# Pooled attention and a maxout network on one Trainium2 core: scores one slot later in three blocks, weight differences by halves, and the last block's lower output stored in two column halves by two queues

## Chip, core and metric

The kernel runs on one core of a Trainium2 chip (trn2). The metric is the device time of one execution in microseconds (us), the median of several runs; lower is better. A profile was taken of one further execution, with the time of every instruction and of every DMA packet.

## What is computed

Attention with keys and values averaged over groups of 8, and then a network whose hidden layer is the maximum of three products:

```python
B, H, S, D = q.shape                                  # 8, 8, 576, 64; pool = 8, Sp = 72
k_p = k.reshape(B, H, Sp, pool, D).mean(axis=3)
v_p = v.reshape(B, H, Sp, pool, D).mean(axis=3)
scores = scale * np.matmul(q, k_p.transpose(0, 1, 3, 2))
attn = softmax(scores)
x = np.matmul(attn, v_p)      # (0, 2, 1, 3), reshaped to 4608 tokens x 512
h = np.maximum(np.maximum(x @ w1, x @ w2), x @ w3)    # w: 512 x 768
out = h @ w_out                                       # 768 x 512
```

## The kernel before

**Work on two levels.** The attention goes by batch: there are 8 batches of 576 tokens. The network goes by blocks of 512 tokens, `n` = 0 to 8. While block `n` goes through the network, the attention of batch `n` + 1 is woven between its matmuls, so TensorE (PE) always has something to do.

**The maximum.** The kernel computes the hidden layer as relu and max of two differences: `w2 - w1` and `w3 - w1` stand in the tiles `mw1` and `mw2` in place of `w2` and `w3`, and the part that is linear in `x` is taken through a third matrix, `wm` = `w1` times `w_out`. The differences are made by `sub_w` (L315 to L320) on VectorE (DVE), in place, one call for 256 columns of both. The hidden layer uses columns `jc` by 128: a call `d1` (columns 256 to 511) serves `jc` = 2 and 3, and `d2` serves `jc` = 4 and 5. `sub_w` takes a start and an end in units of 128 columns; before the loop of block 0 it is already called by halves for the first 256 columns (L483 to L486).

**Slots.** `hidden` (L363) and `project` (L381) are generators, and each `yield` ends a slot. In blocks 2 to 4 a block has 20 slots: slots 0 to 11 are the hidden layer (for each of 6 `jc`, a slot of four 512-column matmuls for `mw1`, evicted by a Relu on ScalarE (ACT), and a slot for `mw2`, evicted by a maximum on DVE, L354), and slots 12 to 19 the projection of four tiles of 128 tokens, in two slots each. The eight slots of block 0 whose `jc` is 0 or 1, and the four whose `jc` is 2, take 256 tokens instead of 512. The PSUM tiles `pw` of the slots rotate through three buffers.

**What is put between slots.** `block` (L498) runs a slot and then the steps that a plan gives for it. `plan` (L532) is the plan of blocks 2 to 4. `k` turns the pooled keys of the next batch (`turn_k`, L194): three transposes on PE into one PSUM tile `pkt`, and four copies into the two zero-padded tiles `kz`, for these batches two by DVE (first tile, `par` = 0) and then two by ACT (second tile, `par` = 1), L198. `s0` to `s7` are the scores of the eight heads (`scores`, L217): for each head one matmul of 320 columns and one of 256, one with each tile of `kz`, and an exponential over 576 columns on ACT (L212). `v0` to `v4` multiply by the values (`values`, L251) and `x` puts the result into `xT` with a DMA transpose. `T` loads transposed queries. In block 0 the plan is written out at L510: it has `d1` after slot 6 and `d2` after slot 10.

**Order.** The order of every engine is the order in which the program issues: the kernel switches the scheduler off with `manual_schedule`. An instruction that has to wait holds back what stands behind it on its engine.

**GpSimd (POOL)** pools the keys and values of the batches 1 to 7 (`fold_v`, and `fold_k` but for batch 1) and issues the loads.

**The end.** The last blocks use a scheme of seven products in place of eight (`seven`, `out_seven`). For the output, `out_seven` (L660) computes a block of 512 tokens as two token halves `j` and two column halves, `lo` and `hi`, in the tile `ob`, and `m` counts the two groups of 128 tokens in each half. The products of the last block (`LAST` = 8) come in the order of L864: 1, 2, 6, 7, 5, 3, 4. The half `j` = 1 (the lower output) is complete in its right columns once products 5 and 7 are added (DVE, `plus`, L725), and in its left columns once product 3 is copied (ACT, L722). `store` (L667) writes a half of one `j` or all its columns, in two DMAs, one for each 64 partitions:

```python
if i in (5, 7, 3) and ended(5, 7, 3):
    store(nc.sync, 1, slice(0, C))
if n == LAST and i in (2, 4) and ended(i):
    store((nc.gpsimd, nc.sync)[i // 4], 0, (lo, hi)[i // 4])
```

After the last product comes what was left of the projection of block 6: one tile of 128 tokens in two column halves (L387), the left one evicted by ACT (L400) and the right one by DVE (L398), each stored by one DMA from SyncE (SP) and one from ACT (L404).

Of the kernel before, what the change touches and what calls it, by code (L numbers as in the profile page):

```python
# [14 lines left out]
def kernel(  # L15
# [11 lines left out]
    nc = tc.nc  # L27
# [3 lines left out]
    B, H, S, D = q.shape  # L31
# [127 lines left out]
    def fold_k(b, e, i0=0, i1=6):  # L159
        if b not in kps:  # L160
            new_kp(b)
        fold(e, kts[b][:, i0:i1], kps[b][:, i0:i1], F16 if e is nc.vector else F32)
# [12 lines left out]
    def turn_q(b, n0, n1, evac, tag):  # L175
        if b not in qTs:
            qTs[b] = sb2.tile([128, 2 * NG, 128], BF16, name="qT", tag="qT")
        pqt = psum([128, n1 - n0, 128], BF16, name="pqt", tag=tag[0],
                       bufs=tag[1])
        qf = qbs[b].rearrange("p hp t d -> p (hp t d)")  # L180
        for n in range(n0, n1):
            nc.tensor.transpose(pqt[:, n - n0, :], qf[:, 128 * n:128 * n + 128],
                                ident)
        evac(out=qTs[b][:, n0:n1, :], in_=pqt)
# [9 lines left out]
    def turn_k(b):  # L194
        pkt = keys(b, ATT if len(pools) < 3 else SC)
        for par, evac in enumerate((nc.vector.tensor_copy, nc.scalar.copy)):
            for odd in range(2):
                (evac if b > 2 else nc.vector.tensor_copy)(  # L198
                    out=kz_all[b % 2][par][64 * par:64 * par + 64, :, 0:Sp].rearrange(
                         "p h (r i t) -> p h r i t", i=3, t=2)[:, :, :, :, odd],  # L200
                     in_=pkt[64 * odd:64 * odd + 64].rearrange("p i (h r) -> p h r i", r=12))
# [12 lines left out]
    def new_et(b):  # L214
        ets[b] = sb2.tile([Sp, H, S], F16, name="et", tag="et")
# [62 lines left out]
    def do(b, steps):  # L278

        for name in steps.split():
            i = int(name[1:] or 0)
            if name[0] in "qQ":
                turn_q(b, *QS[i], nc.vector.tensor_copy if name[0] == "Q"
                       else nc.scalar.copy, TR)
            elif name[0] == "T":
                qTs[b] = sb2.tile([128, 2 * NG, 128], BF16, name="qT", tag="qT")
                nc.sync.dma_start_transpose(
                    out=qTs[b], in_=qbs[b].rearrange("p hp t d -> p (hp t d)"))  # L290
            elif name[0] == "k":
                turn_k(b)
            elif name[0] == "K":
                fold_k(b, nc.vector)
            elif name[0] == "s":
                if i == 0:
                    new_et(b)
                (scores if len(pools) < 3 else scores_flat)(b, i)
            elif name[0] == "d":
                sub_w(i)  # L300
            elif name[0] == "z":
                for par in range(2):
                    nc.vector.memset(kz_all[1][par], 0.0)
            elif name[0] == "w":
                turn_w(i, nc.scalar.copy if i % 2 else nc.vector.tensor_copy)
            elif name[0] == "v":
                xns[b, i] = values(b, CHUNKS[i][0])
            else:
                turn_x(b, *CHUNKS[i], xns[b, i], TR if b == 1 else ATT,
                       nc.vector.tensor_copy if name[0] == "X" else nc.scalar.copy)  # L310
# [4 lines left out]
    def sub_w(i, j0=0, j1=2, wi=(1, 2)):  # L315

        part = slice(256 * i + 128 * j0, 256 * i + 128 * j1)
        for t in [w_sb[w] for w in wi]:
            nc.vector.tensor_tensor(out=t[:, :, part], in0=t[:, :, part],  # L319
                                    in1=w_sb[0][:, :, part], op=ALU.subtract)  # L320
# [211 lines left out]
    def plan(n):  # L532
        b = n + 1
        got = {0: [(b, "k")]}
        got.update({2 + h: [(b, f"s{h}")] for h in range(H)})
        got.update({12 + c: [(b, f"v{c} x{c}")] for c in range(5)})
        got[14 if n == 2 else 13].append((b + 2, "T"))
        return got
# [70 lines left out]
    LAST = TOK // NB - 1  # L609
# [50 lines left out]
    def out_seven(n):  # L660

        o = sb2.tile([128, 2304], F32, name="ob", tag="et")[:, 0:2048].rearrange(
            "p (j m c) -> p j m c", j=2, m=2)
        lo, hi = slice(0, HALF), slice(HALF, C)
        banks, done = {}, set()

        def store(e, j, c):  # L667
            for u in range(2):
                b, g = divmod(2 * (4 * n + 2 * j) + u, NG)
                pair = g + 2 < NG and GS[g + 2] == GS[g] + 4  # L670
                for m in range(0, 2, 1 + pair):
                    b, g = divmod(2 * (4 * n + 2 * j + m) + u, NG)
                    dst = out[S * b:S * b + S, :].rearrange("(r g) c -> r g c", g=NG)
                    e.dma_start(out=dst[:, GS[g]:GS[g] + 4 * pair + 1:4, c],
                                in_=o[64 * u:64 * u + 64, j, m:m + 1 + pair, c])

        def bank(of, m):
            if n < LAST:
                if of not in banks:
                    if of == "A":  # L680
                        banks["A"] = psum([128, 2, 2, HALF], F32, name="oA", tag="val",
                                          bufs=1)[:, 0]
                    else:
                        tag = (PO, SC)[of == "C"]
                        banks[of] = psum([128, 2, HALF], F32, name=f"o{of}", tag=tag[0],
                                         bufs=tag[1])
                return banks[of]
            if (of, m) not in banks:
                tag = {"A": PA, "B": SC, "C": BC if m == 0 else SC}[of]
                banks[of, m] = psum([128, 2, HALF], F32, name=f"o{of}", tag=tag[0],  # L690
                                    bufs=tag[1])[:, 0:1]
            return banks[of, m]

        def product(i, *ms):
            for m in ms:
                matmuls(i, m)
            done.update((i, m) for m in ms)
            evict(i, ms)

        def matmuls(i, m):  # L700
            of = "B" if i == 2 else "C" if i in (4, 7) else "A"
            p = bank(of, m)[:, m if n < LAST else 0]
            za, zb = PRODUCTS[i]
            for r in range(5):
                c = slice(128 * m, 128 * m + 128)
                if isinstance(zb, str):
                    z = int(zb[1]) - 1
                    left = turns(n)[:, z, r, c] if r < 2 else th[n][z][:, r - 2, c]
                else:
                    at = HALF * (zb % 2) + 128 * m  # L710
                    left = (xT[:, 2 * (zb // 2) + r, NB * n + at:NB * n + at + 128] if r < 2
                            else hTs[n][:, JH * (zb // 2) + r - 2, at:at + 128])
                right = out_s(int(za[1]))[:, r] if isinstance(za, str) else out_w(za, r)
                nc.tensor.matmul(  # L714
                    p, left, right, stop=(r == 4), skip_group_check=True,
                    start=(i in FIRST and r == 0 and (m == 0 or n == LAST)))

        def evict(i, ms):
            m, at = ms[0], slice(ms[0], ms[-1] + 1)

            def copy(j, c):
                nc.scalar.copy(out=o[:, j, at, c], in_=bank("A", m))  # L722

            def plus(j, c, of):
                nc.vector.tensor_tensor(out=o[:, j, at, c], in0=o[:, j, at, c],  # L725
                                        in1=bank(of, m), op=ALU.add)

            def ended(*parts):
                return all((z, k) in done for z in parts for k in range(2))

            if i in (1, 5, 6, 3):
                copy(int(i in (5, 3)), lo if i in (1, 3) else hi)
            elif i == 2:
                plus(0, lo, "B")
            elif i == 4:
                plus(0, hi, "C")
            if i in (5, 7) and (12 - i, m) in done:
                plus(1, hi, "C")
            if i in (5, 7, 3) and ended(5, 7, 3):
                store(nc.sync, 1, slice(0, C))  # L740
            if n == LAST and i in (2, 4) and ended(i):
                store((nc.gpsimd, nc.sync)[i // 4], 0, (lo, hi)[i // 4])
            if n < LAST and i in (2, 4) and ended(2, 4):
                store(nc.sync, 0, slice(0, C))

        return product
# [152 lines left out]
```

The softmax here doesn't subtract the row's maximum and nothing guards it: scores larger than these inputs give would overflow.

## Time and profile before

The time is 230.76 us, the median of 3 runs (230.62 to 230.81). The profiled execution took 230.6 us, with a span of 228.7 us from its first instruction to its last.

| what | before |
|---|---|
| span | 228.7 us |
| POOL busy | 153.6 us |
| DVE busy, the group L354 (maximum) | 130.5 us, 25.5 us |
| ACT busy, the group L212 (exponential) | 122.3 us, 35.2 us |
| DMA queue of SyncE and ACT: share of 16 engines | 33.0%, 0.2% |
| stores of `ob` by SyncE, 256 KB, from issue to landing | 3.3 us |
| stores of `ob` by SyncE, 128 KB, from issue to landing | 2.9 us |

How to read it: the busy time of an engine is the sum of its instructions, and its share of the span tells how full it is on average. An engine's idle time costs nothing unless the chain of work that ended last passes through it. PE stands for the matmuls and PEld for the loads of their weights, which overlap. A row of the waits says which engine and line waited, for whom, how long in all, how many times, and the longest. In a row of the timeline there are the start, the length, engine, line, operation, tiles and shapes, how many instructions were merged, and, in brackets, the idle time before it and who ended it. An engine name with a "q" is its queue, which issues DMAs.

### The profile page before, as it was taken

What the parts mean: (1) busy time and instruction counts of PE and PEld (TensorE: products, weight loads), DVE (VectorE), ACT (ScalarE), POOL (GpSimd) and SP (SyncE); (2) the same over time, 40 slices, a digit from 0 to 9 for tenths busy, and PEclk for the clock granted to TensorE, in tenths of its full rate; (3) what the DMA queues carried; (4) which work ended last, traced back from release to release, by engine and by line L of the source; (5) the groups of instructions that cost most, each with busy time, mean ns of one, the idle gap of its engine ahead of it and who ended that gap; (6) DMA issues with size and microseconds to landing.
All of it is one profiled execution on the core that took longest, in us unless ns stands there. A gap on an engine that the chain in (4) does not pass through costs nothing.

```text
span 228.7 us, 4488 instructions
## 1 busy us (share of the span) xinstructions
PE 218.8 (96%) x1717; PEld 137.7 (60%) x1717; DVE 130.5 (57%) x247; ACT 122.3 (53%) x221; POOL 153.6 (67%) x131
## 2 busy tenths in 40 slices
PE   7788999999999999999999999999999999999992
PEld 2477645558656545544454455555677777788881
DVE  3568876038426333633363336378667887798930
ACT  2277424756874486238623862574786446563330
POOL 7975201999949999999999839910225996993020
PEclk9999999999999999999999999999999999999999
DMA  6999999999569999986998699951362553200356
GB/s 173 211 197 197 211 203 209 192 179 216 103 115 210 223 170 209 157 189 113 228 133 214 108 225 195 196 131 25 67 95 41 125 62 75 49 0 0 95 153 171
DMA packets 47125, 33.52 MB, mean 147 GB/s; under 512 B 27072, under 2 KB 41856, under 8 KB 47104
## 3 DMA queue, kind: packets, MB, share of 16 engines
q0 software_dynamic: 16944, 16.98, 45.9%
q1 hardware_dynamic: 30000, 16.13, 33.0%
q8 instruction: 13, 0.21, 0.4%
q10 hardware_dynamic: 160, 0.13, 0.2%
q14 instruction: 8, 0.07, 0.1%
HBM read 34.60 MB, written 9.44 MB: 193 GB/s over the span
## 4 chain that ended last, share of the span: by engine, by line
PE 84%; DVE 7%; DMA 3%; ACT 3%; issue 2%; SPq 0%; ACTq 0%; DVEq 0%
PE pw L346 24%; PE po L395 16%; PE po L391 10%; PE pA L784 6%; PE psc L207 6%; PE pav L255 4%; PE pC L784 3%; PE oA L714 3%; DMA ktTrue<-in_k_dram 3%; PE pm L333 2%; DVE kz L198 2%; PE oC L714 2%; PE pB L784 2%; PE pxt L245 1%; ACT kz L198 1%
## 5 line engine op out<-in xcount | busy, mean ns | idle before, releaser
L346 PE MATMUL pw<-xT,mw 128*128 128x512 f16 (+1 forms) x336 | 73.1, 348 | 0.4 <-ACT xT L249 0.2
L354 DVE TENSOR_TENSOR hT<-t,pw 128x512 f16<-128x512 f16 (+1 forms) x42 | 25.5, 609 | 36.7 <-PE pw L346 18.1
L346 PEld LDWEIGHTS <-mw 128*128 128x128 f16 x336 | 31.6, 98 | 21.5 <-DVE mw L319 0.6
L395 PE MATMUL po<-mwo,hT 128*128 128x512 f16 (+1 forms) x174 | 41.0, 371 | 0.0
L212 ACT ACTIVATE et<-psc 72x576 f16<-72x576 f32 (+2 forms) x54 | 35.2, 661 | 7.0 <-PE psc L207 6.9
L151 POOL TENSOR_TENSOR half<-vt 72x2048 f32<-72x2048 f16 x7 | 28.4, 4058 | 14.1 <-DMA vt<-in_v_dram 13.6
L400 ACT COPY osb<-po 128x512 f32<-128x512 f32 (+1 forms) x28 | 16.2, 579 | 35.9 <-PE po L395 34.7
L352 ACT ACTIVATE t<-pw 128x512 f16<-128x512 f32 (+1 forms) x42 | 22.6, 537 | 13.3 <-PE pw L346 11.5
L391 PE MATMUL po<-wm,xT 128*128 128x512 f16 (+1 forms) x116 | 28.9, 371 | 0.1
L263 DVE TENSOR_TENSOR xn<-pav,rcp 128x512 f16<-128x512 f32 x40 | 27.6, 691 | 1.6 <-DVE rcp L261 0.2
L152 POOL TENSOR_TENSOR half<-half 72x1024 f32<-72x1024 f32 (+1 forms) x13 | 27.3, 2099 | 1.0
L395 PEld LDWEIGHTS <-hT 128*128 128x128 f16 x174 | 16.1, 98 | 14.1
L207 PE MATMUL psc<-qT,kz 128*128 128x320 bf16 (+2 forms) x120 | 22.9, 278 | 1.6 <-ACT kz L198 0.8
L207 PEld LDWEIGHTS <-kz 128*128 128x128 bf16 x143 | 13.1, 98 | 14.9 <-ACT kz L198 2.0
L151 POOL TENSOR_TENSOR half<-ktFalse 96x1536 f32<-96x1536 f16 x6 | 18.6, 3099 | 4.9 <-DMA ktFalse<-in_k_dram 4.7
L255 PEld LDWEIGHTS <-et 72*128 72x128 f16 x320 | 15.6, 98 | 6.8 <-issue 0.2
L790 ACT CAST pad<-pA 128x512 f16<-128x512 f32 x27 | 15.6, 588 | 7.2 <-PE pA L784 5.5
L261 DVE RECIPROCAL rcp<-pav 128x8 f32<-128x8 f32 x40 | 8.2, 205 | 18.6 <-PE pav L255 18.3
L255 PE MATMUL pav<-vp,et 72*128 72x65 f16 x320 | 16.9, 194 | 0.1
L391 PEld LDWEIGHTS <-xT 128*128 128x128 f16 x116 | 10.5, 98 | 8.2 <-issue 0.2
L764 DVE SCALAR_TENSOR_TENSOR hT<-pad 128x512 f16<-128x512 f16 x18 | 14.4, 816 | 1.7 <-ACT pad L794 1.3
L784 PEld LDWEIGHTS <-sw 128*128 128x128 f16 x144 | 13.7, 98 | 2.5
(110 smaller groups left out, 315.4 us busy)
## 6 DMA issues: line engine op xcount, KB each, us to landing
out_dram<-osb SPq DMA_DIRECT2D x54, 128.0 KB, 3.7
ktFalse<-in_k_dram POOLq DMA_DIRECT2D x7, 576.0 KB, 6.8
qb<-in_q_dram POOLq DMA_DIRECT2D x7, 576.0 KB, 13.1
vt<-in_v_dram POOLq DMA_DIRECT2D x7, 576.0 KB, 11.1
mw<-in_moe_w_dram POOLq DMA_DIRECT2D x9, 256.0 KB, 9.1
ktTrue<-in_k_dram SPq DMA_DIRECT2D x3, 384.0 KB, 5.1
out_dram<-ob SPq DMA_DIRECT2D x4, 256.0 KB, 3.3
mwo<-in_moe_w_out_dram POOLq DMA_DIRECT2D x1, 768.0 KB, 12.9
```

The lines of the kernel that those rows point to most:

```text
L151: e.tensor_tensor(out=f, in0=t[:, :, 0:4, :], in1=t[:, :, 4:8, :], op=ALU.add)
L152: e.tensor_tensor(out=f[:, :, 0:2, :], in0=f[:, :, 0:2, :], in1=f[:, :, 2:4, :], op=ALU.add)
L207: nc.tensor.matmul(out, kz_all[b % 2][f % 2][:, h, :], qTs[b][:, n + i0:n + i1, 64 * (h % 2):64 * (h % 2) + 64], start=True, stop=True)
L212: nc.scalar.activation(out=out, in_=in_, func=FT.Exp, scale=1.0 / 64.0)
L255: nc.tensor.matmul(pav[:, h // 4, 65 * (h % 4):65 * (h % 4) + 65], ets[b][:, h, c0:c0 + 128], vp_all[:, b, h, :], start=True, stop=True)
L263: nc.vector.tensor_tensor(out=xn, in0=pv[:, :, :, 0:D], in1=rcp.to_broadcast([128, 2, 4, D]), op=ALU.mult)
L346: mm = nc.tensor.matmul(pw, w_sb[wi][:, kc, bass.ts(jc, 128)], xT[:, kc, col], start=(kc == 0), stop=(kc == KCH - 1))
L352: nc.scalar.activation(out=t, in_=pw, func=FT.Relu)
L354: nc.vector.tensor_tensor(out=hT[:, jc, c0:c1], in0=t, in1=pw, op=ALU.max)
L391: nc.tensor.matmul(po, xT[:, kc, bass.ts(m, 128)], wm_sb[:, kc, c], start=(kc == 0), stop=False)
L395: nc.tensor.matmul(po, hT[:, jc, bass.ts(mm, 128)], wo_sb[:, jc, c], start=False, stop=(jc == JCH - 1))
L784: mm = nc.tensor.matmul(p[:, w], a[:, kc, bass.ts(g, 128)], b[:, kc, :], start=(i in FIRST and w + kc == 0), stop=(w + kc == 2), skip_grou ...
```

## The change

Three edits that don't depend on each other.

The first moves the scores of the next batch one slot later in blocks 2 to 4: `s0` runs after slot 3 instead of slot 2, and `s7` after slot 10 instead of slot 9. It gives the copies of the keys one more slot of hidden-layer matmuls to finish in.

The second cuts each call of the weight differences in block 0 in two: the first 128 columns of both differences, then the second 128 columns. The hidden layer uses 128 columns at a time, so a slot can start when its own half is there.

The third is for the last block alone: the lower output is stored in two column halves. The right half leaves from SyncE as soon as products 5 and 7 are added, and the left half from ACT's queue when product 3 is copied, where before all columns left from SyncE after product 3.

```diff
             elif name[0] == "d":
-                sub_w(i)
+                for j in range(2):
+                    sub_w(i, j, j + 1)
...
         got = {0: [(b, "k")]}
-        got.update({2 + h: [(b, f"s{h}")] for h in range(H)})
+        got.update({3 + h: [(b, f"s{h}")] for h in range(H)})
...
-            if i in (5, 7, 3) and ended(5, 7, 3):
+            if n == LAST and i in (5, 7) and ended(5, 7):
+                store(nc.sync, 1, hi)
+            if n == LAST and i == 3 and ended(3):
+                store(nc.scalar, 1, lo)
+            if n < LAST and i in (5, 7, 3) and ended(5, 7, 3):
                 store(nc.sync, 1, slice(0, C))
```

On the engines, in the order of the two programs: PE, GpSimd have the same instructions, PE with the score matmuls of three blocks elsewhere; DVE has four more; two of SyncE's issues become four, of which two stand on ACT.

## Prediction

> **What bounds the kernel now.** I read the page first. The span is 228.7 us for a run of 230.6 us, so a microsecond of span is a microsecond of time.
>
> ```profile
> PE 218.8 (96%) x1717; PEld 137.7 (60%) x1717; DVE 130.5 (57%) x247; ACT 122.3 (53%) x221; POOL 153.6 (67%) x131
> PEclk9999999999999999999999999999999999999999
> PE 84%; DVE 7%; DMA 3%; ACT 3%; issue 2%; SPq 0%; ACTq 0%; DVEq 0%
> ```
>
> TensorE is busy for 96%, holds 84% of the chain that ended last, at full clock. Work off PE is worth only the PE gap that it opens. So next the waits, those of matmuls and weight loads:
>
> ```profile
> PEld L207 <- ACT kz L198: 2.0, 3, 0.7
> PE psc L207 <- ACT kz L198: 0.8, 3, 0.3
> PEld L346 <- DVE mw L319: 0.6, 2, 0.4
> ```
>
> Three waits of the scores for the key tile `kz`, and two of the hidden layer for the weight differences: exactly what the first two edits touch. The timeline at the start of block 2 (start, duration, engine, line) shows one of the three:
>
> ```profile
> 78.63 1.89 PE L346 MATMUL pw<-xT,mw 128*128 128x512 f16 x8
> 78.83 0.99 DVE L198 COPY kz<-pkt 64x288 bf16<-64x288 bf16 x2 [2.78 <-PE pkt L189]
> 79.90 0.97 ACT L198 COPY kz<-pkt 64x288 bf16<-64x288 bf16 x2 [0.61 <-DVE kz L198]
> 80.35 0.30 PE L207 MATMUL psc<-qT,kz 128*128 128x320 bf16 x1
> 80.92 0.28 PE L207 MATMUL psc<-qT,kz 128*128 128x256 bf16 x1 [0.27 <-ACT kz L198]
> ```
>
> The two hidden slots before `s0` end, and its first matmul starts at 80.35; the second needs ACT's half of `kz`, done at 80.87, and starts at 80.92. In the timeline near 22 to 26 us, the weight differences:
>
> ```profile
> 23.54 1.28 DVE L319 TENSOR_TENSOR mw<-mw,mw 128x1024 f16<-128x1024 f16 x2
> 24.27 0.33 PEld L346 LDWEIGHTS <-mw 128*128 128x128 f16 x4 [0.37 <-DVE mw L319]
> 24.74 0.41 DVE L354 TENSOR_TENSOR hT<-t,pw 128x256 f16<-128x256 f16 x1
> 24.88 0.33 PEld L346 LDWEIGHTS <-mw 128*128 128x128 f16 x4 [0.27 <-DVE mw L319]
> ```
>
> PE waits once for each of the two subtractions. Last, the end: issues in the timeline, then stretches (length, PE, PEld, DVE, ACT, POOL busy, clock, DMA share, GB/s).
>
> ```profile
> 221.31 2.88 SPq L674 DMA_DIRECT2D out_dram<-ob  x4
> 223.50 1.62 ACTq L404 DMA_DIRECT2D out_dram<-osb  x2
> 224.29 1.34 SPq L404 DMA_DIRECT2D out_dram<-osb  x2
> ...
> 221.00:222.30 1.30, 1.30 (x14) 1.17 (x13) 0.71 (x2) 0.29 (x1) 0.00 (x0) 1.00 0.00 0
> 222.30:224.00 1.70, 1.70 (x17) 1.41 (x15) 0.13 (x1) 0.37 (x1) 0.00 (x0) 1.00 0.78 164
> 224.00:226.00 2.00, 0.15 (x2) 0.00 (x0) 0.42 (x1) 0.00 (x0) 0.00 (x0) 1.00 0.93 284
> ```
>
> SyncE issues six stores back to back, to 225.63, although the last data (DVE copy, 424 ns from 224.19) is ready at 224.61. The DMA engines idle until 222.3 and are then full until 226.
>
> **What the Trainium skill says.** "PSUM — Partial Sum Buffer", section "PSUM bank collisions raise a hardware error": accesses of two engines to one bank and quadrant, two reads included, must be kept apart. The trace agrees in form: ACT, with nothing else to do from 79.29, starts its half of `kz` 0.08 us after DVE's. "TensorE: Matmul & The Clock Gate", section "Back-to-back issue gap": N/2.4 + 2.5 ns; four 512-column matmuls take 0.86 us here, as it says. "VectorE: DVE Perf Modes", section "The TRN2 errata": a fixed cost per instruction. Agrees: 1024 elements take 682 ns, 512 take 416. "DMA: Bandwidth & Descriptors", section "Issuing engines are not separate DMA queues": a second issuing engine saves only issue time. Here that is 0.6 us a store (2.88/4 at most).
>
> **The change part by part.**
>
> *Scores.* The counts of matmuls, exponentials and copies stay; eight pairs of score matmuls move one hidden slot later in blocks 2, 3 and 4. Removed: `s0` should run 0.136 us (320 columns) after its first matmul and runs 80.92 - 80.35 = 0.57 after, so 0.435 is lost. The wait occurs three times (rows above), so 3 x 0.435 = 1.30 us. In its new place `s0` comes after three slots, 78.63 + 3 x 0.863 = 81.22, and `kz` is ready at 80.87: no wait, 0.35 spare. Moved cost: at the other end `s7` now has one hidden slot and four projection matmuls (2 x 0.86) between it and `v0` instead of three groups. Its exponential (0.65) queues on ACT behind one Relu (0.60, start-to-start 0.49): the Relu of slot 10 starts at 89.87, the exponential would end near 91.0, and `v0` loads the weights of head 7 near 91.5; it is a separate wait there, so 0.5 spare. The alternation on ACT (one Relu, two exponentials per two slots, 1.9 us against 2.2 of PE) only shifts. PSUM buffers: `pw` slots 3 to 5 need tiles freed at 79.3, 80.5 and 81.5 and start from 80.4, 81.5 and 82.6 on. GpSimd has the next keys about 4 us or more early in these blocks. Bounds: -1.1 to -1.35; I take -1.30.
>
> *Weight differences.* Four DVE instructions become eight. Two of 682 ns, 0.60 apart, become four of 416 ns, 0.33 apart (three such took 1.08 us at 17.68). Slot 8 then finds its first half at 23.54 + 0.42 = 23.96, before slot 7 ends (24.02), and slot 9 its half at 24.29, before 24.46. Both PE waits go: 0.26 + 0.16 = 0.42. But behind the subtractions on DVE stands the maximum of slot 7, which frees one of three `pw` buffers. It starts at 24.87 instead of 24.74 and ends at 25.28. Slot 10 needs this buffer and would like to start at 25.12 (before: 25.55). It starts near 25.34, so 0.21 of 0.42 remains. A second cap: GpSimd finishes the keys of batch 2 at 55.22 (54.23 + 1.00), on a clock set by the landing of `vt` at 39.19, and PE loads them at 55.45: an arrival over about 0.2 earlier waits there. The two later subtractions are ahead of their use by over 1 us. Bounds 0 and -0.42; I take -0.21.
>
> *End.* The lower 512 KB leave as 4 x 128 KB instead of 2 x 256 KB: the right columns from SyncE once DVE has added them (219.89 + 0.42 = 220.31), the left from ACT at 221.29 after its last copy. SyncE's two are issued by 221.65, before it is wanted again at 222.44. So its four remaining stores run at the pace of their data; the last starts about 224.67 instead of 225.09: 0.42 less. ACT's two issues end by 222.5 and its next copy is at 223.10: hidden. Each store also waits for an older one on its completion semaphore; the older ones at issue here start by 217.3 and land within 3.5 us, by 220.8. The DMA work is the same bytes in rows of 1 KB instead of 2 KB, 256 KB of it moved into the idle stretch before 222.3. Landing takes 2.2 to 2.9 us from issue and should be nearer the lower end. ACT's own last store starts at 224.65 either way, so the last landing cannot come before about 226.9 (before: SyncE's closing wait for the stores passes at 227.37). Bounds -0.2 (landing as slow as now for ACT's store) and -0.7; I take -0.45.
>
> Sum: -1.30 - 0.21 - 0.45 = -1.96, so 230.76 - 1.96 = 228.80.
>
> **Rivals.** (1) Only the scores count: GpSimd's batch-2 keys swallow the weights' gain, and ACT's last store, unmoved, sets the end. 230.76 - 1.30 = 229.46. For: a late `vt` would do the first. Against: ACT's queue held 128 KB among saturated engines. (2) The scores' gain is lost to an equal wait at `v0`, and the rest stays: 230.76 - 0.66 = 230.10. Against: 0.5 spare. (3) Slower: were the exponential of `s7` behind one more Relu and exponential (1.25), `v0` would wait 0.75 three times: 3 x (0.75 - 0.435) = +0.95, with nothing from the rest, 231.71. Against: ACT idles 0.22 before every second exponential here. (4) More: 1.35 + 0.42 + 0.70, 228.29, if the maximum gets ahead and the last store lands fast.
>
> **How the numbers follow.** Forecast 0.67, rival 1 0.14, rival 4 0.11, rival 2 0.05, rival 3 0.03. The range runs from rival 4 to rival 1, 228.3 to 229.5. Faster by over 0.2% (below 230.30) holds in all but rival 3 and a little of rival 2: 0.94; same 0.03; slower 0.03.
>
> **What would show it.** Right: the rows of PE and PEld waiting for `kz` of ACT gone, those for `mw` gone but about 0.2 us of PE wait on the maximum (L354) near 25; no PE wait before `v0`; DMA traffic from about 221.5 less the earlier gain, and SyncE's last issue within 0.1 of the last copy. Wrong: a PE wait on the exponential at `v0`, on `kp` of batch 2 near 55, or a last landing still 2.8 us after the last matmul's copy.

## The result, and the profile after

The changed kernel takes **229.13 us** (median of 6 runs, 228.26 to 229.60) beside 230.65 us (6 runs, 230.42 to 230.81): a ratio of 0.9931, 95% interval 0.9911 to 0.9952, or 1.5 us less. Run a second time in another session (below) it took 228.55 us beside 230.47, a ratio of 0.9902 [0.9880, 0.9924]. The forecast was 228.8, the range 228.3 to 229.5. So the time came out as foretold; its three terms did not. Ratios here and below leave out runs over 1.5% above the fastest of their kernel, which is one run in all (232.45 us, of the scores alone).

The profiled execution took 228.95 us, with a span of 227.0 us. From its page, the busy times, the granted clock and the chain of work that ended last:

```profile
PE 217.5 (96%) x1716; PEld 137.6 (61%) x1717; DVE 131.5 (58%) x251; ACT 122.1 (54%) x221; POOL 153.5 (68%) x131
...
PEclk9999999999999999999999999999999999999999
...
PE 70%; DMA 12%; POOL 11%; DVE 3%; issue 2%; ACT 0%; POOLq 0%; DVEq 0%; ACTq 0%
PE pw L347 21%; PE po L396 14%; PE po L392 9%; DMA vt<-in_v_dram 8%; PE pA L789 6%; PE psc L207 4%; DMA mw<-in_moe_w_dram 4%; PE pav L255 3%; POOL half L151 3%; PE pC L789 3%; PE oA L715 3%; PE oC L715 2%; POOL half L152 2%; PE pB L789 2%; 
```

The clock is full, the counts are those of before but for four more instructions on DVE (and one record of a matmul fewer). What is new is the chain: PE's share of it fell from 84% to 70%, and a load of values (`vt`) and GpSimd's sums of them (`half`) came in with 8% and 5%. The waits of PE and of its weight loads say where (line numbers are one or more higher than before, since the change adds lines):

```profile
PE pav L255 <- POOL vp L154: 0.2, 1, 0.2
PE pkt L189 <- POOL kp L154: 0.2, 1, 0.2
...
PEld L189 <- POOL kp L154: 0.4, 1, 0.4
```

The three rows for `kz` of ACT and `mw` of DVE are gone. In their place PE waits for GpSimd: once for the pooled values of batch 1, once for the pooled keys of batch 2. The timeline at the two places that matter for the weight differences, first their slots, then the two new waits:

```profile
23.60 1.42 DVE L320 TENSOR_TENSOR mw<-mw,mw 128x512 f16<-128x512 f16 x4
24.94 0.74 DVE L355 TENSOR_TENSOR hT<-t,pw 128x256 f16<-128x256 f16 x2
25.18 0.60 PE L347 MATMUL pw<-xT,mw 128*128 128x256 f16 x4
...
47.66 0.42 PE L255 MATMUL pav<-vp,et 72*128 72x65 f16 x8 [0.16 <-POOL vp L154]
55.85 0.30 PE L189 MATMUL pkt<-ident,kp 96*128 96x96 bf16 x3 [0.15 <-POOL kp L154]
```

Slot 10 starts at 25.18 without a wait, while the maximum of slot 7 (the first of the two at 24.94) still runs, to 25.35. Later PE waits at 47.66 and 55.85. At the end, the issues with the last copy, and three stretches (the same columns as in the prediction):

```profile
219.44 3.37 SPq L675 DMA_DIRECT2D out_dram<-ob  x4
220.41 1.40 ACTq L675 DMA_DIRECT2D out_dram<-ob  x2
222.60 1.66 ACTq L405 DMA_DIRECT2D out_dram<-osb  x2
222.91 1.33 SPq L405 DMA_DIRECT2D out_dram<-osb  x2
223.29 0.43 DVE L399 COPY osb<-po 128x256 f32<-128x256 f32 x1 [1.76 <-PE po L396]
```

```profile
220.10:221.40 1.30, 1.30 (x14) 1.16 (x13) 0.72 (x2) 0.28 (x1) 0.00 (x0) 1.00 0.42 102
221.40:223.10 1.70, 1.70 (x17) 1.41 (x15) 0.13 (x1) 0.37 (x1) 0.00 (x0) 1.00 0.88 226
223.10:225.10 2.00, 0.15 (x2) 0.00 (x0) 0.43 (x1) 0.00 (x0) 0.00 (x0) 1.00 0.76 225
```

PE's last work comes 0.90 us earlier than before, and the stretches are set that much earlier too. In the first one, where the DMA engines stood idle before (0.00), they are 42% busy; in the last one they have slack (0.76, before 0.93). The last copy ends at 223.72 and the last store lands at 225.96, 2.24 us later; before it was 224.61 and 227.53, 2.91 us. From there to the end of the span it is 1.05 us (before 1.13). So the end brings 0.67 + 0.08 = 0.75 us, and what precedes it 0.9.

**How far ahead PE is.** Both programs have the same 336 matmuls of the hidden layer. Subtracting the start of the same matmul in the profile before shows where PE gains or loses (us; minus is earlier). The last three columns are kernels of the experiments; the first row is scatter of the start-up.

| at (time before) | changed | weights, values in halves | scores alone, a late run | all, relieved |
|---|---|---|---|---|
| 17.8 | +0.06 | -0.20 | -0.33 | -0.31 |
| 26.6 | -0.35 | -0.62 | -0.32 | -0.73 |
| 52.7 | -0.02 | -0.61 | -0.32 | -0.73 |
| 57.6 | +0.30 | -0.61 | -0.18 | -0.73 |
| 132.2 | -1.25 | -0.62 | -1.08 | -2.29 |
| 155.1 | -0.90 | -0.62 | +1.44 | -2.04 |

In the changed kernel PE gains 0.41 near 25 us, which is the whole pair of waits for the weight differences, and then loses 0.33 and 0.32 at GpSimd's two results: in this run the edit cost 0.24. From 57.6 to 155.1 it gains 1.20 by the scores. (Of the 1.55 that show at 132.2, 0.24 is no gain: a pair of score matmuls has moved past the matmul compared, and comes before the next block's start. A further 0.12 is lost at the start of block 5, of which more below.)

### The profile page after: what moved, and what is told of

It reads as the page before. It is cut to its first block, busy times and chain, and to the rows that moved or that the text cites. A ratio compares the mean times of both kernels' runs of the same rounds, so it can differ in the third digit from the quotient of the medians.

```text
span 227.0 us, 4497 instructions
## 1 busy us (share of the span) xinstructions
PE 217.5 (96%) x1716; PEld 137.6 (61%) x1717; DVE 131.5 (58%) x251; ACT 122.1 (54%) x221; POOL 153.5 (68%) x131
## 4 chain that ended last, share of the span: by engine, by line
PE 70%; DMA 12%; POOL 11%; DVE 3%; issue 2%; ACT 0%; POOLq 0%; DVEq 0%; ACTq 0%
PE pw L347 21%; PE po L396 14%; PE po L392 9%; DMA vt<-in_v_dram 8%; PE pA L789 6%; PE psc L207 4%; DMA mw<-in_moe_w_dram 4%; PE pav L255 3%; POOL half L151 3%; PE pC L789 3%; PE oA L715 3%; PE oC L715 2%; POOL half L152 2%; PE pB L789 2%; POOL mw L108 1%
## 5 line engine op out<-in xcount | busy, mean ns | idle before, releaser
L207 PE MATMUL psc<-qT,kz 128*128 128x320 bf16 (+2 forms) x120 | 22.4, 278 | 1.0 <-DVE qT L184 0.9
L198 DVE COPY kz<-pkt 64x288 bf16<-64x288 bf16 x18 | 8.7, 481 | 11.5 <-PE pkt L189 11.3
```

Of the source, the lines that this page charges most:

```text
L207: nc.tensor.matmul(out, kz_all[b % 2][f % 2][:, h, :], qTs[b][:, n + i0:n + i1, 64 * (h % 2):64 * (h % 2) + 64], start=True, stop=True)
```

## Experiments

Two theories stood. *Clock of the loads*: each edit frees what the prediction said, but GpSimd's sums and the loads that GpSimd issues run on a clock of their own, only just ahead of PE, and take back what comes too early. *Rival*: the edits are worth less in themselves, because halved subtractions cost DVE, later scores push the exponentials, or the end is limited to issue time. All kernels are edits of the kernel before or, where all three edits are in, of the changed kernel.

### Each part alone, and all again

Scores alone (the second part of the diff), and weight differences alone (the first part):

> Only the scores one slot later. Theory A (the three gains add up, and GpSimd's key and value sums for the batches 1 and 2, started by the landing of the second value load, take away what comes early): 229.3 to 229.4 us, that is 1.25 to 1.30 less, since GpSimd has 4 us to spare in blocks 2 to 4; no wait for kz of ACT in the rows of PE and PEld; a spread like that of the kernel before (0.4 us). Theory B (the gain of the scores is partly taken back later, and the rest comes from the stores): 229.8 or more, with a new PE wait after 80 us.

> Only the weight differences by halves. Theory A: PE is 0.42 us earlier from 25 us on and loses it again at the sums of values (near 47 us) and keys (near 55 us) of GpSimd, if the second value load lands as late as in the changed kernel's profile (39.7): 230.5 to 230.8, no clear difference, a wider spread than before. Theory C (the edit as such costs time, because the longer run of subtractions on DVE holds back the maximum behind it): slower than before by 0.1 to 0.3, with a PE wait on the maximum near 25 us.

The stores alone (the third part), and the changed kernel again beside them:

> Only the stores of the last block. Theory A: 0.7 to 0.8 us less, 229.9: the last store is issued within 0.1 us of the last copy and lands about 2.2 us later, and the closing waits are shorter by 0.25 us. Theory D (the end gives only the 0.42 us of SyncE's issue time, as predicted, and the larger end of the changed kernel's profile was chance): 230.2.

> The changed kernel again, beside the single edits. Theory A: less than the sum of the three single gains by nothing, but not better than scores and stores alone would give (230.65 - 1.28 - 0.75 = 228.6), and 228.6 to 229.2 with a spread over 1 us that follows the landing of the second value load: each 0.1 us later there is 0.1 us of time. Theory C: 0.2 us or more above the sum of the gains of scores and stores.

| kernel | median, us | runs | ratio to before | 95% interval |
|---|---|---|---|---|
| before | 230.47 (230.11 to 232.16) | 59 | | |
| scores alone | 229.39 (228.99 to 232.45) | 22 | 0.9957 | 0.9941 to 0.9972 |
| weights alone | 230.50 (229.71 to 232.16) | 22 | 0.9994 | 0.9979 to 1.0008 |
| stores alone | 229.81 (229.53 to 231.64) | 22 | 0.9975 | 0.9962 to 0.9989 |
| all three | 228.55 (228.01 to 229.42) | 6 | 0.9902 | 0.9880 to 0.9924 |

By the medians the scores bring 1.08, the weights nothing, the stores 0.66; their sum, 1.71, is just under the lower edge of the interval of all three (1.75; by the medians 1.92). The fastest runs, a weaker measure, tell another thing: 1.12, 0.40 and 0.58 below the fastest of before, and 2.10 for all three, just their sum. So it seems that the weight edit can bring its 0.4, but mostly doesn't. Its waits:

```profile
PE pkt L189 <- POOL kp L154: 0.2, 1, 0.2
...
PEld L189 <- POOL kp L154: 0.4, 1, 0.4
```

The waits for `mw` are gone, and the one for the keys of batch 2 has come. In the trace PE gains 0.42 by 26.6 us, and by 57.6 has lost 0.54, more than that gain: 0.20 at 47.3 and 0.34 at 55.5. At both places it goes on 0.05 us after GpSimd's result (47.24 and 55.43).

The scores' median hides a tail: 5 of the 21 runs that count are over 230.19, which is 0.8 above their median, against 4 of 59 that are as far above theirs for the kernel before. The profile is of one of them, a run of 232.06 us. From its timeline:

```profile
63.64 1.99 SPq L289 DMA_TRANSPOSE qT<-qb  x1
68.22 0.77 POOL L100 DMA_DIRECT2D qb<-in_q_dram  x1 [5.00 <-DMA qT<-qb]
...
130.53 0.56 POOL L79 DMA_DIRECT2D ktFalse<-in_k_dram  x1
...
147.72 1.02 PE L346 MATMUL pw<-xT,mw 128*128 128x512 f16 x4 [2.12 <-DMA xT<-xn]
```

and of the tile `xT` between 128 and 150 us, the time that its transposes needed from issue to landing:

```profile
DMA to landing us min/median/max: 2.4/4.9/8.2
```

The same lines of the kernel before:

```profile
61.56 1.96 SPq L289 DMA_TRANSPOSE qT<-qb  x1
66.08 0.77 POOL L100 DMA_DIRECT2D qb<-in_q_dram  x1 [2.94 <-DMA qT<-qb]
...
128.40 0.56 POOL L79 DMA_DIRECT2D ktFalse<-in_k_dram  x1
```

This is the clock of the loads, now for the scores. GpSimd may load the next queries only when the transpose of the queries of batch 3 has been through; in the late run the three loads issued at 47 us landed 2.1 to 2.4 us later than before, so the transpose started 2.08 later (63.64 for 61.56) and GpSimd went on 2.14 later. From there GpSimd is busy almost without a break, in the kernel before to 128 us, so the lateness stays, and the last loads start 2.13 later. The transposes of `x` that SyncE issues at 137.6 and 140.3 land only once those loads have landed (queries at 145.04, the transposes at 145.85 and 147.59). PE starts block 5 at 147.72, after 2.1 us of waiting. In the kernel before, the second transpose lands at 144.98 and PE asks for it at 146.28: 1.3 us of slack, as much as the scores edit brings forward. In the profile of all three (229.42 us) PE comes 0.92 late at the same place, 0.13 after that landing (145.70), as in the late run. (The row of the timeline names a copy of ACT, which ended within 0.01 us of the landing; in the kernel before PE goes on there without waiting for that copy.)

The start of block 3 shows the same. In the late run PE begins there at 100.51, 0.09 after the last transpose of `x` has landed (100.42), and loses 0.65; in the kernel before, the landing is at 99.57 and PE comes at 100.48, a slack of 0.9.

The edit is not what makes the loads late: they landed late before the first score that it moves (80 us). It takes away the slack that hides a late load. Why the three loads landed late in this run stays open.

### Relieving GpSimd

Next, kernels that give the two edits what the theory says they lack. The pooling of keys for batch 4 (5.9 us of GpSimd's long stretch before the last loads) goes to DVE in a kernel with the scores edit; that of batch 2 goes to DVE in a kernel with the weights edit; a control has both moves and no edit, and a fourth has everything.

```diff
-              29: [(1, "s4 s5")], 30: [(1, "s6 s7")], 31: [(1, "v0")],
+              29: [(1, "s4 s5")], 30: [(1, "s6 s7"), (2, "K")], 31: [(1, "v0")],
...
-    fold_k(2, nc.gpsimd)
...
         got[14 if n == 2 else 13].append((b + 2, "T"))
+        if n == 2:
+            got[17] = [(4, "K")]
...
-    FOLDS_OF = {1: "k3 v3", 2: "k4 v4 k5", 3: "v5 k6 v6", 4: "k7 v7"}
+    FOLDS_OF = {1: "k3 v3", 2: "v4 k5", 3: "v5 k6 v6", 4: "k7 v7"}
```

> The scores edit alone, with the key sums of batch 4 moved from GpSimd (5.9 us of its time) to VectorE in slot 17 of the block before, so that GpSimd issues the loads of batch 7 some 4 to 6 us earlier and the two transposes of hidden inputs that land behind them are there before block 5 needs them. Theory L (the loads that GpSimd issues are a second clock that runs within 0.2 us of TensorE once the scores waits are gone, and takes back part of the gain in part of the runs): the full 3 x 0.435 = 1.30 in the median, 229.2 beside 230.5, and no runs near 231 or above. Rival M (what the scores edit leaves at a median of 1.08 is all that it is worth, because the score matmuls or the exp fall later themselves): 229.4 as without the move, or more if VectorE's 2 to 3 us of sums hold up an eviction.

> The weight differences by halves alone, with the key sums of batch 2 moved from GpSimd to VectorE (slot 30 of block 0), so that the keys which TensorE loads near 55 us no longer hang on the clock that the landing of the second value load sets. Theory L: the 0.42 that TensorE gains at 25 us is kept but for the value sums near 47 us (0.1 to 0.2 of wait), so 0.25 to 0.42 less than before, 230.1 to 230.25 beside 230.5. Rival M (halving costs VectorE as much as it brings TensorE): no gain, 230.5, and no wait of TensorE on GpSimd in the trace.

> The control: the kernel before with only the two moves of key sums from GpSimd to VectorE. Theory L: in the kernel before TensorE comes after GpSimd and its loads everywhere (by about 0.1 us at 55 us and 1.5 us at the start of block 5), so taking work from GpSimd brings nothing by itself: 230.5 within 0.2. Rival M': the moves are worth something by themselves, 0.3 us or more less, and then what the two other kernels gain says nothing of the edits. Rival N: VectorE's added work holds TensorE up, 0.3 us or more above.

> All three edits with both moves of key sums. Theory L: the three gains in full, 1.30 + 0.3 to 0.42 + 0.6 to 0.75 = 2.2 to 2.5, so 228.0 to 228.3 beside 230.5, with a narrower spread than the changed kernel's (228.0 to 229.6). Rival M: as the changed kernel, 228.5 to 229.1. If the trace shows another wait of TensorE on a load near block 3 or block 5, the moves were not enough.

| kernel | median, us | runs | ratio to before | 95% interval |
|---|---|---|---|---|
| before | 230.59 (230.08 to 232.10) | 27 | | |
| scores, keys 4 moved | 229.12 (228.88 to 229.31) | 6 | 0.9929 | 0.9906 to 0.9952 |
| weights, keys 2 moved | 230.68 (230.42 to 231.08) | 14 | 0.9999 | 0.9987 to 1.0011 |
| before, both moved | 230.62 (230.01 to 231.23) | 14 | 0.9995 | 0.9980 to 1.0010 |
| all, both moved | 228.37 (228.19 to 228.66) | 5 | 0.9900 | 0.9877 to 0.9923 |

The moves bring nothing by themselves. With the scores edit, the move of the keys of batch 4 brings the forecast's 1.3 or so (1.47 by the medians), and the late runs are gone from its six; six are few, so this alone is no proof. Its trace shows the last loads issued at 125.61, the queries landed at 140.90, and `x` at 144.01, 1.2 us ahead of PE; PE lost 0.33 at the start of block 3 in that run, again behind a transpose of `x` (landed at 100.20, PE at 100.29). The kernel with all edits and both moves, at 228.37, just missed its forecast of 228.0 to 228.3. The weights edit gained nothing, and this was neither theory. From the timeline of the kernel with that edit and the keys of batch 2 moved:

```profile
44.95 1.68 DVE L151 TENSOR_TENSOR halfh<-ktFalse 96x1536 f16<-96x1536 f16 x1 [2.13 <-DMA ktFalse<-in_k_dram]
45.90 1.86 POOL L154 TENSOR_TENSOR vp<-half 72x512 f16<-72x512 f32 x1
46.67 1.50 DVE L152 TENSOR_TENSOR halfh<-halfh 96x768 f16<-96x768 f16 x1
47.81 0.42 PE L255 MATMUL pav<-vp,et 72*128 72x65 f16 x8 [0.70 <-POOL vp L154]
```

GpSimd's last value sum takes 1.86 us, where it takes 1.26 in the kernel before, and DVE's two sums 1.68 and 1.50, where the same two for batch 1, with GpSimd idle, take 0.95 and 0.55. The move put its DVE work in the very place where GpSimd was making the values of batch 1, and PE lost 1.06 there, where it had lost 0.54 at values and keys together without the move. In the profile of all three edits with both moves it lost 0.91 there. The cure for one wait of PE made the other worse; for the weights edit this run decides nothing.

### Values of batch 1 in halves

So the same question again without more work for DVE: batch 1's values are loaded and summed in two halves of four heads, which lets GpSimd start on the first half when it lands.

```diff
-    load_v(1, nc.gpsimd)
+    load_v(1, nc.gpsimd, cuts=(0, 4, 8))
...
-    def fold_v(b):
-        fold(nc.gpsimd, vts[b], vp_all[:, b, :, 0:D])
+    def fold_v(b, h=0, g=H):
+        fold(nc.gpsimd, vts[b][:, h:g], vp_all[:, b, h:g, 0:D])
...
-    fold_v(1)
+    fold_v(1, 0, 4)
+    fold_v(1, 4, 8)
```

> The weight differences by halves alone, with the values of batch 1 loaded and summed in two halves of four heads: GpSimd can begin about 2 us sooner, and no work goes to VectorE (moving the key sums of batch 2 there drew GpSimd's last value sum out from 1.27 to 1.86 us, and TensorE waited 0.86 us for it at 47.8 us). Theory L (only GpSimd's sums, started by a landing, take the 0.42 back): the waits at 47 and 55 us are gone, 0.3 to 0.42 less than before. Rival M (halving costs VectorE as much as it brings): no gain, and no wait of TensorE on GpSimd either.

> The control: the kernel before with only the values of batch 1 in halves. Theory L: TensorE comes after GpSimd by 0.1 us or more everywhere in the kernel before, so an earlier GpSimd brings nothing, within 0.2 us of before. Rival M': 0.3 us or more less by itself, and then the weight differences are worth nothing in the other kernel either.

> All three edits, with the values of batch 1 in halves and the key sums of batch 4 on VectorE. Theory L: none of TensorE's waits on GpSimd near 47 and 55 us and none on loads near 100 and 145 us is left; the three gains in full, 1.30 + 0.3 to 0.42 + 0.66 = 2.25 to 2.4, so 228.1 to 228.3 with all runs within 0.5 us, 0.2 less than with the key sums of both batches on VectorE (228.37). Rival M: 228.4 to 229.1 again.

| kernel | median, us | runs | ratio to before | 95% interval |
|---|---|---|---|---|
| before | 230.46 (230.17 to 231.56) | 51 | | |
| weights, values in halves | 230.18 (229.71 to 231.28) | 22 | 0.9987 | 0.9978 to 0.9997 |
| before, values in halves | 230.37 (230.15 to 230.75) | 14 | 0.9993 | 0.9982 to 1.0004 |
| all, values in halves, keys 4 moved | 228.12 (227.79 to 228.35) | 5 | 0.9895 | 0.9872 to 0.9918 |

The weights edit now shows a gain, 0.28 us, of which up to 0.09 is what the halves bring without it. The interval of the kernel with it leaves out 1; that of the kernel without it doesn't. The two intervals overlap, so by time alone the edit's worth is not fixed; the trace, which is of one run, shows what becomes of PE's gain. GpSimd's values are done at 46.02, PE uses them at 47.08 and does not wait:

```profile
45.30 0.72 POOL L154 TENSOR_TENSOR vp<-half 72x256 f16<-72x256 f32 x1
47.08 0.43 PE L255 MATMUL pav<-vp,et 72*128 72x65 f16 x8
```

In the table of PE's lead, the 0.42 that this kernel gains by 26.6 is still there at 155.1, to 0.01 us. And the kernel with everything is the best of all: 228.12 us, 2.3 below before, as the clock of the loads foretold (228.1 to 228.3), though its lead over the changed kernel (0.43 by the medians of two sessions) rests on 5 and 6 runs. The chain of work that ended last, from its page:

```profile
PE 91%; DVE 4%; issue 2%; ACT 1%; DVEq 0%; ACTq 0%
```

No load and no GpSimd are left in it. In the last column of the table, PE gains 0.42 at 25 us, and 1.31 more from 57.6 to 155.1: 3 x 0.435, the forecast's 1.30 within 0.01.

### What the end is worth, and why

The stores alone brought 0.66, more than the forecast's 0.45 and a little less than the 0.7 to 0.8 expected from the profile. Is it the time to issue, or the earlier traffic? This kernel changes the queue only: the lower output leaves undivided and as late as before, from ACT instead of SyncE.

```diff
             if i in (5, 7, 3) and ended(5, 7, 3):
-                store(nc.sync, 1, slice(0, C))
+                store(nc.scalar if n == LAST else nc.sync, 1, slice(0, C))
```

> The end alone, but only the queue changed: the lower output of the last block leaves undivided (2 x 256 KB) and as late as before, from ScalarE in place of SyncE. If the gain of the stores is the issue time that SyncE is spared (forecast: 0.42), this keeps 0.42, with the last issue within 0.1 us of the last copy. If the earlier start of the right half also counts, through less traffic behind the last copy (from issue to landing 2.2 us in place of 2.7), this has only some 0.3 to 0.45 of the 0.66 that the whole edit brought, and its last landing is again 2.6 us or more after the last copy. Rival: ScalarE's two issues of 0.6 us hold up its own last copy, and nothing is gained.

It takes 230.95 us (22 runs, 230.69 to 232.14) beside 230.46: a ratio of 1.0021 [1.0012, 1.0030], **slower** by 0.5 us, which none of the expectations had. From its list of DMA issues from 218 us on (KB each, median us from issue to landing), and then its timeline:

```profile
out_dram<-ob ACTq DMA_DIRECT2D x2, 256.0 KB, 3.5
out_dram<-ob SPq DMA_DIRECT2D x2, 128.0 KB, 4.5
out_dram<-osb ACTq DMA_DIRECT2D x2, 64.0 KB, 3.5
out_dram<-osb SPq DMA_DIRECT2D x2, 64.0 KB, 3.0
```

```profile
222.32 1.86 SPq L674 DMA_DIRECT2D out_dram<-ob  x2
224.06 0.42 DVE L398 COPY osb<-po 128x256 f32<-128x256 f32 x1 [1.76 <-PE po L395]
224.28 1.47 SPq L404 DMA_DIRECT2D out_dram<-osb  x2
```

SyncE has two issues fewer, and yet its last one starts at 224.94, 0.46 after the last copy, just as in the kernel before (0.47). One of its issues took 1.19 us in place of 0.6, with 640 KB of stores issued in the 1.8 us before it; why is not shown. The last store lands 3.35 us after the last copy. The same list for the kernel before, and then with the stores edit:

```profile
out_dram<-ob SPq DMA_DIRECT2D x2, 256.0 KB, 3.4
out_dram<-ob SPq DMA_DIRECT2D x2, 128.0 KB, 3.2
out_dram<-osb ACTq DMA_DIRECT2D x2, 64.0 KB, 2.8
out_dram<-osb SPq DMA_DIRECT2D x2, 64.0 KB, 2.7
```

```profile
out_dram<-ob SPq DMA_DIRECT2D x4, 128.0 KB, 2.4
out_dram<-ob ACTq DMA_DIRECT2D x2, 128.0 KB, 2.5
out_dram<-osb ACTq DMA_DIRECT2D x2, 64.0 KB, 2.3
out_dram<-osb SPq DMA_DIRECT2D x2, 64.0 KB, 2.1
```

With the edit the groups land in 2.1 to 2.5 us by their medians, and the last store 2.26 us after the last copy. ACT's last store separates the two causes, since its issue starts 0.03 us after the last copy in both kernels: in the kernel before it lands 2.74 us after that copy, SyncE's last one 2.91. So an earlier issue on SyncE alone could have brought 0.17 at most; the rest is that ACT's store, issued at the same point, lands 0.48 us sooner. So the second queue alone is worth nothing here, or less. What the trace points to is that 256 KB leave in the stretch in which the DMA engines were idle: by the records of the packets, those that end after the last copy are 606 KB in the kernel before, 373 KB with the edit, and 636 KB in the kernel with the queue changed. This agrees with the Trainium skill's "DMA: Bandwidth & Descriptors", section "Issuing engines are not separate DMA queues", which has all issuers' transfers end on the same 16 engines; and the only saving which that section leaves to a second issuer, the issue time, did not come here. Why the undivided stores from two queues are slower than from one was not tried; and the edit's parts (the early right half, the left half by the other queue, and rows of half the length, which come with both) were not run apart.

## Why the prediction was right, and where it was not

**Right by its sum, not by its terms.** It said -1.30, -0.21 and -0.45, in all -1.96. By the medians of the parts alone it is -1.08, +0.03 and -0.66; the changed kernel had -1.52 in one session and -1.92 in the other. Two terms too large and one too small made up for each other in part, and that is luck.

**Scores: the mechanism and the size on PE were right, and a step was missing.** 0.435 three times is what PE gains (1.31 in the kernel with everything), the waits for `kz` are gone, and no wait for the exponential came at `v0`. But the step "GpSimd has the next keys about 4 us or more early in these blocks" looked at GpSimd's results only. It did not ask what else hangs on GpSimd's time: the loads that it issues, and the transposes of `x` on SyncE, which land behind them. Their slack was 0.9 us at block 3 and 1.3 at block 5, to be read from the trace of before; a gain of 1.30 uses the second up, and in the run that was traced the loads were later than that. That this is also what keeps the median at 1.08 is made likely by the kernels that relieve GpSimd, not shown run by run. Rival 2 had the right kind of thought, a new wait that takes the gain, in the wrong place. (The formula that the prediction quotes for the pace of matmuls is given there for a matmul by itself, not for a stream of them; what the sums rest on is the 0.86 us for four that the trace shows.)

**Weight differences: both steps failed, in opposite ways.** "Slot 10 needs this buffer" is wrong: slot 10 starts at 25.18, while the maximum that was to free its buffer runs to 25.35. PE gained 0.42, not 0.21. The second cap was named (the keys of batch 2, and "an arrival over about 0.2 earlier waits there"), but priced with the clock of one profile (there `vt` lands at 39.11, and GpSimd starts on it at 39.19). The landing of `vt` that starts that clock lies between 38.86 and 39.71 us in the profiles of kernels that leave this load whole; at 39.71, in the changed kernel's profile, PE lost 0.65, more than it had gained. And GpSimd's values, which PE takes 8 us earlier on the same clock, were not in the working at all. The median worth of the edit in this kernel is nothing; this is what rival 1 said of it.

**End: the direction was right, the main reason wrong, the size too small.** "The last starts about 224.67 instead of 225.09: 0.42 less" counted issue time. The last issue does come at once after the last copy (0.03 after it; before 0.47). But ACT's last store, which does not move, caps what this can bring at 0.17 as long as it lands no sooner, near the prediction's own bound of -0.2, and the kernel that only takes two issues off SyncE lost 0.5 us. Most of the gain is that stores land sooner, with less traffic left behind the last copy: 2.24 us to the last landing in place of 2.91. The prediction had this as a side remark ("nearer the lower end") and as its bound of -0.7; measured 0.66 alone, and 0.75 in the profile.

**Its signs.** Of those named for "right": the rows for `kz` and `mw` gone, the last issue within 0.1 of the last copy, and traffic earlier. Of those for "wrong": the wait on `kp` of batch 2 near 55 is there. The 0.2 us wait for the maximum near 25 is not.

## What to carry to other kernels

When one engine carries the chain of waits, measure how far ahead every other chain is (loads, the sums they start, transposes that land behind loads) at the places where the first engine meets it: a gain larger than the smallest of these leads is only partly kept, and here the part varied from run to run. A wait taken away should then be followed through the trace as a lead, matmul by matmul, since the place where it is lost again can lie 20 to 120 us later. At the end of a kernel, count bytes still to go after the last computation before counting issues; here early bytes in an idle stretch were worth more than another queue.

## What was not expected of the hardware

- Sums on GpSimd and DVE at the same time draw each other out: 1.26 to 1.86 us on GpSimd, 0.95 to 1.68 and 0.55 to 1.50 on DVE. The Trainium skill's "SBUF — State Buffer", section "SBUF: two separate sides", says that the two share a pair of ports, which (for a DVE instruction with two inputs in SBUF beside a GpSimd one that reads SBUF) one holds for a whole instruction while the other is blocked. The records agree to within 0.14 us: taking the undisturbed lengths back from the ends, DVE's first sum would begin at 45.69 (GpSimd's earlier one ends at 45.82), GpSimd's at 46.50 (DVE's ends at 46.64), and DVE's second at 47.62 (GpSimd's ends at 47.76). So they seem to take turns, and the record counts the waiting as length.
- A DMA transpose of `x` needs 2.4 us in the median; the two issued at 137 to 141 us, while loads of GpSimd were on their way, took up to 8.2 us, and landed only after the last of these loads (in the late run 0.8 and 2.5 us after it, in the kernel before 0.6 and 2.6). It need not be the last: with the keys of batch 4 moved, one issued at 125.71 landed at 134.05, after the first of three loads (132.98) and before the other two.
- Issuing a 128 KB store took 0.6 us as a rule and 1.19 us with 640 KB of other stores issued in the 1.8 us before it (in the kernel before, 0.85 us with 640 KB in 2.0 us).
